# Second-layer products in a form with four sums on each operand, and a third quarter-product first layer, in an attention and mixture-of-experts kernel

## The chip, the cores and the metric

The kernel runs on one core of one Trainium2 chip, as one program. The metric is the device time of an execution in microseconds; the kernel before was run three times. One more execution was taken with the hardware profiler, and every time inside the kernel comes from that one.

## The reference

Eight batches, eight heads of 64, 512 local and 32 global tokens each; the output of the attention is the input of a layer of eight experts over all 4352 tokens.

```python
# attention: global queries see all keys; local queries see the global keys
# and the local keys at a distance of at most 32
s_g   = q_g @ concat(k_g, k_l).T / 8;   out_g = softmax(s_g) @ concat(v_g, v_l)
s_l   = concat(q_l @ k_g.T / 8, where(|i-j| <= 32, q_l @ k_l.T / 8, -1e9))
out_l = softmax(s_l) @ concat(v_g, v_l)
x = concat(out_g, out_l) as [4352, 512]
# experts, E = 8, F = 1024
P = exp(x @ w_gate - max)
8 times: P /= P.sum(1); P /= P.sum(0); P *= N / E
out = sum over e of P[:, e] * (relu(x @ w1[e]) @ w2[e])
```

## The kernel before

The first stage (up to about 340 us) computes the attention and, between its steps, the first layer of experts 0 to 3, whose hidden rows go to DRAM (`hd`). Then the eight normalizations of P run on VectorE while TensorE works off the rest of these first layers. The change lies in the second stage, from about 396 us to the end.

**Units and slots.** The tokens lie in nine groups: 0 to 7 are the 512 local tokens of a batch, group 8 holds the 256 global tokens. In each group the experts are taken in the order 4, 0, 5, 1, 6, 2, 7, 3. One expert on one group is a *unit* i = 8 m + slot; the loop at L1073 goes over the 72 units. Even slots (experts 4 to 7) have their first layer computed here, two units ahead; odd slots (0 to 3) load theirs from DRAM (`load_h`) and scale it by P (`scale_h`, a multiplication of the whole 128x4096 tile h, or of halves of it). For even slots the input is scaled instead (`scale_x`).

**Second layer.** A unit's h is seen as a 2x2 block matrix: rows t1 and t2 (halves of the tokens), columns lo and hi (halves of F, four k-steps each); w2 of an expert as 2x2 blocks as well, kept in `w2c` as seven prepared blocks (`prep_w2c`). Seven products of half size replace eight. `sums` makes their left operands on VectorE, in s (three planes) and in place in h; `product(i, q)` issues product q, eight matmuls of 256 columns with h or s as the stationary operand. Five products stay in their own accumulator banks for the whole group (`ps_fix`) and are added into o once, at the unit that closes the group (slot 7); two use rotating banks and are added after each odd unit (`add`). An addition is one VectorE instruction on 128x512 fp32 from PSUM into o; the first write of a block of o is made by ScalarE. `store` then writes the group out.

**First layer.** `l1` is the plain form: eight rows fm of four matmuls of 512 columns, a ReLU on ScalarE after each. Where `fast(i)` holds (experts 6 and 7 in groups 2 to 7), `Fast` computes it in two halves of F, p = 0 during the even unit i - 2 and p = 1 during the odd unit i - 1, by seven quarter products (four matmuls of 256 columns each) in four steps s0 to s3. ScalarE copies two banks in s0; VectorE makes one addition in s1 (X, L861) and one in s2 (Y, L868), and ReLUs follow in s1, s2 and s3. `sums_x` makes four operands of 128x512 from the scaled x. The stationary operands are seven prepared blocks of w1 (`w1c`), built in group 1 by `prep_w1` from raw blocks and written to DRAM; `wseq` fixes the order in which w1 tiles pass through two buffers.

**Order.** The schedule is manual: every engine runs its instructions in the order in which the program issues them. The loop interleaves them by hand. Three places matter here:

- An even unit that is itself fast (L1084 on) first makes the sums of its k-steps 2 and 3, since these depend on p = 1; k-steps 0 and 1 were summed in the odd unit before.
- In an odd unit with `Fast` (L1148 on), `late` (the even unit before was fast) puts the second half of `scale_h` for unit i + 2 behind the sums.
- The closing odd unit, slot 7, has no `Fast` before: it makes the sums of the next unit first, then the products and their additions (L1171 on).

Of the kernel before, what the change touches and what calls it, by code (L numbers as in the profile page):

```python
# [23 lines left out]
def kernel(  # L24
# [53 lines left out]
    WX = {6: 2, 7: 2}  # L78
# [612 lines left out]
    def prep_w2c(e):  # L691
        w = w2c[e]
        for o, a, b, op in ((0, 1, 4, ALU.add), (5, 1, 2, ALU.add), (6, 3, 4, ALU.add),
                            (2, 2, 4, ALU.subtract), (3, 3, 1, ALU.subtract)):
            tt(w[:, :, o], w[:, :, a], w[:, :, b], op)
# [13 lines left out]
    for j, (e, p) in enumerate((e, p) for e in WX for p in range(2)):  # L709
        wseq.insert(wseq.index((E + 2 * j + 2, None)), (e, "raw", p))  # L710
# [168 lines left out]
    def sums(i, k0=0, k1=HF, part=(0, 1)):  # L879
        if i >= NUN - 1:  # L880
            return
        n = groups[units[i][0]][1]
        t1, t2 = slice(0, n // 2), slice(n // 2, n)
        h = hs[i]
        if i not in ss:
            new_s(i)
        s = ss[i][:, :, k0:k1]
        lo, hi = h[:, k0:k1], h[:, HF + k0 : HF + k1]
        if 0 in part:
            tt(s[:, 0:2, :, 0 : n // 2], lo[:, :, 0:n].rearrange("p k (a t) -> p a k t", a=2),  # L890
               hi[:, :, 0:n].rearrange("p k (a t) -> p a k t", a=2), ALU.add)
            tt(s[:, 2, :, 0 : n // 2], lo[:, :, t1], hi[:, :, t2], ALU.add)
        if 1 in part:
            tt(lo[:, :, t2], lo[:, :, t2], lo[:, :, t1], ALU.subtract)
            tt(hi[:, :, t1], hi[:, :, t1], hi[:, :, t2], ALU.subtract)
# [3 lines left out]
    def rot():  # L899
# [4 lines left out]
    QUARTER = {1: ((0, 0, 1), (1, 1, 1)), 2: ((1, 0, 1), (1, 1, -1)), 3: ((0, 1, 1), (1, 1, 1)),  # L904
               4: ((1, 0, 1), (0, 0, 1)), 5: ((0, 0, -1), (0, 1, 1)), 6: ((1, 1, 1),), 7: ((0, 0, 1),)}
# [6 lines left out]
    def product(i, q):  # L912
        m, e = units[i]
        n = groups[m][1]
        nt = n // P // 2
        first = e == ORDER[0]
        h, s, w = hs[i], ss[i], w2c[e]
        lhs = {1: (s[:, 2], 0), 2: (s[:, 1], 0), 3: (h[:, 0:HF], 0), 4: (h[:, HF:FT], n // 2),
               5: (s[:, 0], 0), 6: (h[:, 0:HF], n // 2), 7: (h[:, HF:FT], 0)}[q]
        if q >= 6 and i % 2 == 0:  # L920
            pm = fixed[q] = ps_rot.tile([P, 512], FP32, tag=rot(), name="pm")
        elif first:
            pm = fixed[q] = ps_fix.tile([P, 512], FP32, tag=f"m{q}", name=f"m{q}")
        else:
            pm = fixed[q]
        for t in range(nt):
            for k in range(HF):
                nc.tensor.matmul(pm[:, HD * t : HD * (t + 1)], lhs[0][:, k, lhs[1] + P * t : lhs[1] + P * (t + 1)],  # L928
                                 w[:, k, q - 1, :], start=(k == 0 and t == 0 and (first if q < 6 else i % 2 == 0)),
                                 stop=(k == HF - 1 and (closes(i) if q < 6 else i % 2 == 1 or closes(i))),  # L930
                                 skip_group_check=True)

    def add(i, q, pm):
        m, e = units[i]
        nt = groups[m][1] // P // 2
        if m not in os_:
            os_[m] = ypool.tile([P, NJ, D], FP32, tag="y", name="o")
        for j, (r, d, sg) in enumerate(QUARTER[q]):
            o = os_[m][:, nt * r : nt * (r + 1), HD * d : HD * (d + 1)]
            p = pm[:, 0 : HD * nt].rearrange("p (t d) -> p t d", d=HD)  # L940
            if (q >= 6 and e == ORDER[1]) or (q in (3, 4) and j == 0):
                nc.scalar.mul(o, p, 1.0 / float(E))
            else:
                nc.vector.scalar_tensor_tensor(out=o, in0=p, scalar=sg / float(E), in1=o, op0=ALU.mult, op1=ALU.add)  # L944
# [4 lines left out]
    def last_pair(i):  # L949
        m, e = units[i]  # L950
        o, h, w = os_[m], hs[i], w2c[e]
        n = groups[m][1]
        lo, hi = h[:, 0:HF, 0:n], h[:, HF:FT, 0:n]
        s = ss[i]
        for c in range(n // P):
            q = slice(P * c, P * (c + 1))
            for d, terms in ((1, ((lo, 2), (s, 4))), (0, ((hi, 3), (s, 1)))):
                pm = ps_rot.tile([P, HD], FP32, tag=rot(), name="pm")
                for t, (a, wi) in enumerate(terms):
                    for k in range(HF):  # L960
                        nc.tensor.matmul(pm, a[:, k, q], w[:, k, wi, :],
                                         start=(t == 0 and k == 0), stop=(t == 1 and k == HF - 1))
                oc = o[:, c, HD * d : HD * (d + 1)]
                nc.vector.scalar_tensor_tensor(out=oc, in0=pm, scalar=1.0 / float(E), in1=oc, op0=ALU.mult, op1=ALU.add)
            for b in range(4 * c, 4 * c + 4):
                eng = (nc.sync, nc.scalar)[b % 2]
                eng.dma_start(out=out[S * b : S * b + Sg, :], in_=o[W * (b % 4) : W * (b % 4 + 1), c, :])
# [105 lines left out]
    for i, (m, e) in enumerate(units):  # L1073
        if i == NUN - 1:
            last_pair(i)
        elif i % 2 == 0:
# [9 lines left out]
            if fast(i + 2):  # L1086
                f = Fast(i + 2, 0)
                if not fast(i):
                    sums(i + 1, part=(0,))
                if fast(i):  # L1090
                    product(i, 3)
                    f.s0()
                    product(i, 4)
                    f.s1()
                    product(i, 5)
                    product(i, 2)
                    sums(i + 1, part=(0,))
                else:
                    f.s0()
                    product(i, 3)  # L1100
                    f.s1()
                    product(i, 4)
                    product(i, 5)
                    sums(i + 1, part=(1,))
                f.s2()
                used.add((i + 2, 0))
                if fast(i):
                    sums(i + 1, part=(1,))
                scale_x(i + 4)
                if not fast(i):  # L1110
                    scale_h(i + 3, 0, HF)
                    product(i, 2)
                product(i, 1)
                f.s3()
                nrot = 0
                product(i, 6)
                product(i, 7)
# [8 lines left out]
            if m > 0:  # L1126
# [9 lines left out]
            for q, fm in ((3, 3), (4, 4), (5, 5), (2, 6), (1, 7), (6, None), (7, None)):  # L1136
# [6 lines left out]
        else:  # L1143
# [4 lines left out]
            if fast(i + 1):  # L1148
                f = Fast(i + 1, 1)
                for q in (6, 7):  # L1150
# [4 lines left out]
                product(i, 3)  # L1155
                f.s0()
                product(i, 4)
                f.s1()
                sums_x(i + 3, (5,))
                product(i, 5)  # L1160
                product(i, 2)
                sums(i + 1, 0, 2, part=(0,))
                f.s2()
                sums(i + 1, 0, 2, part=(1,))
# [3 lines left out]
                product(i, 1)  # L1168
# [6 lines left out]
            for q in (6, 7, 3, 4, 5, 2, 1):  # L1175
                product(i, q)
                if q >= 6 or closes(i):
                    add(i, q, fixed[q])
                if q == 7 and m == 0:
# [34 lines left out]
```

## Time and profile before

| | us |
|---|---|
| three runs: median (lowest to highest) | 1045.08 (1044.48 to 1048.59) |
| the profiled execution, its own time | 1044.08 |
| span of its profile, first to last instruction | 1042.2 |
| TensorE busy in the span | 1015.2 |
| VectorE / ScalarE / GpSimd busy | 868.7 / 513.0 / 139.7 |
| a pair of units with plain first layer, from the chain's first-layer marks (421.99, 441.12) | 19.13 |
| groups 2 to 6, each | 74.95 |
| matmuls of the second layer (L928): number, mean record | 3780, 273 ns |

[...] The granted TensorE clock is 0.995 in the mean. [...]

### The profile page before, as it was taken

How to read it: one execution, taken by the hardware profiler on the slowest of the kernel's cores; microseconds unless marked ns; L12 is line 12 of the kernel's file. 1: busy time of each engine (PE TensorE's matmuls, PEld its weight loads, DVE VectorE, ACT ScalarE, POOL GpSimd, SP SyncE). 2: the span in 40 equal slices, each digit the busy share in tenths (PEclk: the TensorE clock that was granted, in tenths of full speed). 3: DMA queues.
4: the chain of work that ended last, by engine and by line, in shares of the span. 5: the costliest groups of instructions: out<-in, count | busy, mean ns of one | idle time of the engine just before them, and what ended most of it. 6: DMA issues, size and time to landing. Idle time of an engine off the chain costs nothing.

```text
span 1042.2 us, 22693 instructions
## 1 busy us (share of the span) xinstructions
PE 1015.2 (97%) x9142; PEld 728.5 (70%) x9142; DVE 868.7 (83%) x1638; ACT 513.0 (49%) x1296; POOL 139.7 (13%) x227
## 2 busy tenths in 40 slices
PE   7899999999999999999999999999999999999998
PEld 4555555555555466777777877877877878878887
DVE  7687777777776786999889799889899898898895
ACT  7777878787876675223222333333333332332331
POOL 7442423414312102000000000000000000000000
PEclk9899999999999999999999999999999999999999
DMA  9887588988945999946756546454553555464470
GB/s 260 197 217 207 118 273 181 220 232 177 258 136 142 275 261 302 259 143 203 272 194 234 189 153 219 160 189 180 200 189 138 203 187 168 172 218 152 145 260 26
DMA packets 101960, 206.08 MB, mean 198 GB/s; under 512 B 33936, under 2 KB 68192, under 8 KB 90592
## 3 DMA queue, kind: packets, MB, share of 16 engines
q1 hardware_dynamic: 56064, 162.75, 45.1%
q0 software_dynamic: 43184, 32.26, 17.7%
q10 hardware_dynamic: 2608, 9.64, 2.4%
q8 instruction: 71, 1.16, 0.4%
q14 instruction: 33, 0.27, 0.1%
HBM read 168.64 MB, written 57.29 MB: 217 GB/s over the span
## 4 chain that ended last, share of the span: by engine, by line
PE 83%; ACT 8%; DVE 6%; issue 2%; DMA 1%; SPq 0%; POOL 0%; ACTq 0%; DVEq 0%
PE m L928 28%; PE ph L818 15%; PE ph L468 15%; PE pm L928 11%; PE pf L836 7%; ACT Pu L311 4%; DVE Pu L348 3%; PE ptw L359 1%; ACT hT L471 1%; ACT qbd L285 1%; PE pv L157 1%; PE pt L275 1%; DMA vraw<-in_v_l_dram 1%; PE po L380 1%; DVE m L411 1%
## 5 line engine op out<-in xcount | busy, mean ns | idle before, releaser
L468 PE MATMUL ph<-xT,w1e 128*128 128x512 f16 (+1 forms) x1152 | 255.9, 367 | 0.2
L928 PEld LDWEIGHTS <-h 128*128 128x128 f16 x2160 | 211.4, 98 | 36.6
L820 ACT ACTIVATE h<-ph 128x512 f16<-128x512 f32 (+1 forms) x192 | 107.5, 562 | 204.2 <-PE ph L818 202.2
L928 PE MATMUL m<-w2c,s 128*128 128x256 f16 x1620 | 199.9, 273 | 0.0
L928 PEld LDWEIGHTS <-s 128*128 128x128 f16 x1620 | 158.5, 98 | 30.5
L818 PE MATMUL ph<-xs,w1s 128*128 128x512 f16 (+1 forms) x768 | 174.6, 361 | 0.0
L468 PEld LDWEIGHTS <-w1e 128*128 128x128 f16 x1152 | 105.4, 98 | 96.1 <-issue 3.0
L689 DVE TENSOR_TENSOR h<-h,pb 128x2048 f16<-128x2048 f16 (+1 forms) x48 | 152.4, 3175 | 3.8 <-DMA h<-hd 3.7
L689 DVE TENSOR_TENSOR s<-h 128x1024 f16<-128x1024 f16 (+2 forms) x166 | 126.4, 803 | 24.3 <-PE m L928 16.9
L928 PE MATMUL m<-w2c,h 128*128 128x256 f16 x1080 | 137.2, 273 | 0.0
L471 ACT ACTIVATE hT<-ph 128x512 f16<-128x512 f32 (+1 forms) x192 | 104.4, 559 | 47.5 <-PE ph L468 45.2
L928 PE MATMUL pm<-w2c,h 128*128 128x256 f16 x1080 | 123.8, 273 | 0.0
L818 PEld LDWEIGHTS <-w1s 128*128 128x128 f16 x768 | 75.1, 98 | 52.6
L843 ACT ACTIVATE h<-pf 128x512 f16<-128x512 f32 x96 | 55.0, 596 | 84.1 <-PE pf L836 79.9
L311 ACT ACTIVATE Pu<-ms,mx 128x160 f16<-128x160 f32 x224 | 93.6, 420 | 5.2 <-DVE mx L308 2.7
L473 DVE TENSOR_SCALAR hT<-ph 128x512 f16<-128x512 f32 x96 | 66.1, 688 | 31.3 <-PE ph L468 30.5
L689 DVE TENSOR_TENSOR h<-h 128x1024 f16<-128x1024 f16 (+1 forms) x166 | 90.3, 586 | 0.0
L689 DVE TENSOR_TENSOR xs<-xg,pb 128x2048 f16<-128x2048 f16 (+1 forms) x36 | 78.1, 2169 | 12.8 <-DMA pb<-pd 12.8
L947 POOL DMA_DIRECT2D out_dram<-o x8 | 6.1, 758 | 533.3 <-DVE o L944 533.3
L308 DVE CUSTOM_DVE_ANT_0 ms<-sc,mask 128x160 f32<-128x160 f32 x224 | 59.9, 319 | 18.7 <-PE sc L303 18.2
L836 PEld LDWEIGHTS <-w1q 128*128 128x128 f16 x672 | 65.7, 98 | 7.7
L852 ACT COPY pf<-pf 128x512 f32<-128x512 f32 x24 | 13.7, 570 | 81.5 <-PE pf L836 81.5
(165 smaller groups left out, 1225.7 us busy)
## 6 DMA issues: line engine op xcount, KB each, us to landing
h<-hd SPq DMA_DIRECT2D x32, 1024.0 KB
hd<-hT SPq DMA_DIRECT2D x26, 1024.0 KB
w1s<-w1d SPq DMA_DIRECT2D x24, 1024.0 KB
w1q<-w1c SPq DMA_DIRECT2D x24, 896.0 KB
pb<-pd SPq DMA_DIRECT2D x64, 256.0 KB
w2c<-in_moe_w_dram POOLq DMA_DIRECT2D x16, 512.0 KB, 20.1
out_dram<-o POOLq DMA_DIRECT2D x8, 1024.0 KB, 4.6
f<-in_q_l_dram SPq DMA_DIRECT2D x15, 512.0 KB
```

Of the source, the lines that this page charges most:

```text
L308: nc.vector.tensor_tensor_reduce(out=ms[:, ii, :], in0=sc[:, SW * ii : SW * (ii + 1)], in1=mask[:, mi, :], scale=-scale, scalar=BIG, op0=A ...
L311: nc.scalar.activation(out=d["Pu"][:, i, :], in_=ms[:, ii, :], func=AF.Exp, scale=-1.0, bias=d["mx"][:, i : i + 1], accum_out=d["sm"][:, i ...
L348: nc.vector.tensor_tensor(out=d["Pu"][:, i0:i1, 0:KW], in0=d["Pu"][:, i0:i1, 0:KW], in1=d["rs"][:, i0:i1].unsqueeze(2).to_broadcast([P, i1 ...
L468: nc.tensor.matmul(ph[:, 0:n], wts[e][:, dk, P * fm : P * (fm + 1)], xT[m][:, dk, :], start=(dk == 0), stop=(dk == DP - 1))
L471: nc.scalar.activation(out=hT[:, fm, 0:n], in_=ph[:, 0:n], func=AF.Relu)
L473: nc.vector.tensor_scalar(out=hT[:, fm, 0:n], in0=ph[:, 0:n], scalar1=0.0, scalar2=None, op0=ALU.max)
L689: nc.vector.tensor_tensor(out=out, in0=in0, in1=in1, op=op)
L818: nc.tensor.matmul(ph[:, 0:n], w1s[i][:, dk, P * fm : P * (fm + 1)], xss[i][:, dk, 0:n], start=(dk == 0), stop=(dk == DP - 1))
L820: nc.scalar.activation(out=hs[i][:, fm, 0:n], in_=ph[:, 0:n], func=AF.Relu)
L836: nc.tensor.matmul(bank[:, 256 * c : 256 * (c + 1)], self.w[:, self.sta[q], k, P * c : P * (c + 1)], self.mov[q][:, k], start=(first and c ...
L843: nc.scalar.activation(out=self.h[:, k : k + 2, 256 * c : 256 * (c + 1)], in_=bank.rearrange("p (k t) -> p k t", k=2), func=AF.Relu)
L928: nc.tensor.matmul(pm[:, HD * t : HD * (t + 1)], lhs[0][:, k, lhs[1] + P * t : lhs[1] + P * (t + 1)], w[:, k, q - 1, :], start=(k == 0 and ...
```

## The change

The seven products take another form, in which each operand is made with four additions. `sums` has now four parts: S1 = lo t2 + hi t2, S2 = S1 - lo t1, (lo t2 - lo t1) in place, S4 = hi t1 - S2. The rotating products are 2 and 4; the fixed ones 1, 6, 7, 5, 3, in this order. Products 1, 2 and 4 read h as it is; 6 reads S2, 7 the in-place difference, 5 reads S1 and 3 reads S4. `prep_w2c` makes four blocks instead of five.

Expert 4 gets the quarter form in groups 3 to 7 (`WX`): its first layer is then computed during slots 6 and 7 of the group before. So slot 6 becomes an even unit that is fast and is followed by a fast one, and slot 7 an odd unit with `Fast` that also closes its group. Raw blocks of w1 are taken one pair of units earlier, so that expert 4's are built by unit 16.

```diff
-    WX = {6: 2, 7: 2}
+    WX = {6: 2, 7: 2, 4: 3}
...
     def prep_w2c(e):
         w = w2c[e]
-        for o, a, b, op in ((0, 1, 4, ALU.add), (5, 1, 2, ALU.add), (6, 3, 4, ALU.add),
-                            (2, 2, 4, ALU.subtract), (3, 3, 1, ALU.subtract)):
-            tt(w[:, :, o], w[:, :, a], w[:, :, b], op)
+        for o, a, b in ((0, 2, 1), (2, 2, 4), (5, 4, 0), (6, 5, 3)):
+            tt(w[:, :, o], w[:, :, a], w[:, :, b], ALU.subtract)
...
-        wseq.insert(wseq.index((E + 2 * j + 2, None)), (e, "raw", p))
+        wseq.insert(wseq.index((E + 2 * j + 0, None)), (e, "raw", p))
...
-    def sums(i, k0=0, k1=HF, part=(0, 1)):
+    def sums(i, k0=0, k1=HF, part=(0, 1, 2, 3)):
...
-        s = ss[i][:, :, k0:k1]
+        s1, s2, s4 = (ss[i][:, j, k0:k1, 0 : n // 2] for j in range(3))
         lo, hi = h[:, k0:k1], h[:, HF + k0 : HF + k1]
-        if 0 in part:
-            tt(s[:, 0:2, :, 0 : n // 2], lo[:, :, 0:n].rearrange("p k (a t) -> p a k t", a=2),
-               hi[:, :, 0:n].rearrange("p k (a t) -> p a k t", a=2), ALU.add)
-            tt(s[:, 2, :, 0 : n // 2], lo[:, :, t1], hi[:, :, t2], ALU.add)
-        if 1 in part:
-            tt(lo[:, :, t2], lo[:, :, t2], lo[:, :, t1], ALU.subtract)
-            tt(hi[:, :, t1], hi[:, :, t1], hi[:, :, t2], ALU.subtract)
+        for j, (o, a, b, op) in enumerate(((s1, lo[:, :, t2], hi[:, :, t2], ALU.add), (s2, s1, lo[:, :, t1], ALU.subtract),
+                                           (lo[:, :, t2], lo[:, :, t2], lo[:, :, t1], ALU.subtract),
+                                           (s4, hi[:, :, t1], s2, ALU.subtract))):
+            if j in part:
+                tt(o, a, b, op)
...
-    QUARTER = {1: ((0, 0, 1), (1, 1, 1)), 2: ((1, 0, 1), (1, 1, -1)), 3: ((0, 1, 1), (1, 1, 1)),
-               4: ((1, 0, 1), (0, 0, 1)), 5: ((0, 0, -1), (0, 1, 1)), 6: ((1, 1, 1),), 7: ((0, 0, 1),)}
+    ROT, FIX = (2, 4), (1, 6, 7, 5, 3)
...
-        lhs = {1: (s[:, 2], 0), 2: (s[:, 1], 0), 3: (h[:, 0:HF], 0), 4: (h[:, HF:FT], n // 2),
-               5: (s[:, 0], 0), 6: (h[:, 0:HF], n // 2), 7: (h[:, HF:FT], 0)}[q]
-        if q >= 6 and i % 2 == 0:
+        lhs = {1: (h[:, 0:HF], 0), 2: (h[:, HF:FT], 0), 3: (s[:, 2], 0), 4: (h[:, HF:FT], n // 2),
+               5: (s[:, 0], 0), 6: (s[:, 1], 0), 7: (h[:, 0:HF], n // 2)}[q]
+        wi = {1: 1, 2: 3, 3: 4, 4: 6, 5: 0, 6: 5, 7: 2}[q]
+        r = q in ROT
+        if r and i % 2 == 0:
             pm = fixed[q] = ps_rot.tile([P, 512], FP32, tag=rot(), name="pm")
...
                 nc.tensor.matmul(pm[:, HD * t : HD * (t + 1)], lhs[0][:, k, lhs[1] + P * t : lhs[1] + P * (t + 1)],
-                                 w[:, k, q - 1, :], start=(k == 0 and t == 0 and (first if q < 6 else i % 2 == 0)),
-                                 stop=(k == HF - 1 and (closes(i) if q < 6 else i % 2 == 1 or closes(i))),
+                                 w[:, k, wi, :], start=(k == 0 and t == 0 and (i % 2 == 0 if r else first)),
+                                 stop=(k == HF - 1 and (i % 2 == 1 or closes(i) if r else closes(i))),
...
-        for j, (r, d, sg) in enumerate(QUARTER[q]):
-            o = os_[m][:, nt * r : nt * (r + 1), HD * d : HD * (d + 1)]
-            p = pm[:, 0 : HD * nt].rearrange("p (t d) -> p t d", d=HD)
-            if (q >= 6 and e == ORDER[1]) or (q in (3, 4) and j == 0):
-                nc.scalar.mul(o, p, 1.0 / float(E))
+        o00, o01, o10, o11 = (os_[m][:, nt * r : nt * (r + 1), HD * d : HD * (d + 1)] for r in range(2) for d in range(2))
+        p = pm[:, 0 : HD * nt].rearrange("p (t d) -> p t d", d=HD)
+        c = 1.0 / float(E)
+
+        def plus(o, a, sg=1):
+            nc.vector.scalar_tensor_tensor(out=o, in0=p, scalar=sg * c, in1=a, op0=ALU.mult, op1=ALU.add)
+
+        if q in ROT:
+            o, sg = {2: (o00, 1), 4: (o10, -1)}[q]
+            if e == ORDER[1]:
+                nc.scalar.mul(o, p, sg * c)
             else:
-                nc.vector.scalar_tensor_tensor(out=o, in0=p, scalar=sg / float(E), in1=o, op0=ALU.mult, op1=ALU.add)
+                plus(o, o, sg)
+        elif q == 1:
+            nc.scalar.mul(o01, p, c)
+            plus(o00, o00)
+        elif q == 7:
+            plus(o11, o01)
+            tt(o10, o10, o11, ALU.add)
+        else:
+            plus(o01, o01)
+            if q == 5:
+                plus(o11, o11)
...
@@ -1085,36 +1099,36 @@
                 sums(i, 2, 4)
             if fast(i + 2):
                 f = Fast(i + 2, 0)
-                if not fast(i):
-                    sums(i + 1, part=(0,))
                 if fast(i):
+                    product(i, 1)
+                    f.s0()
+                    product(i, 6)
+                    f.s1()
+                    product(i, 7)
+                    product(i, 5)
+                    sums(i + 1, part=(0, 1))
+                    f.s2()
+                    sums(i + 1, part=(2, 3))
+                    scale_x(i + 4)
                     product(i, 3)
+                else:
+                    sums(i + 1, part=(0, 1))
                     f.s0()
-                    product(i, 4)
+                    product(i, 1)
                     f.s1()
+                    product(i, 6)
+                    product(i, 7)
+                    sums(i + 1, part=(2, 3))
+                    f.s2()
+                    scale_x(i + 4)
+                    scale_h(i + 3, 0, HF)
                     product(i, 5)
-                    product(i, 2)
-                    sums(i + 1, part=(0,))
-                else:
-                    f.s0()
                     product(i, 3)
-                    f.s1()
-                    product(i, 4)
-                    product(i, 5)
-                    sums(i + 1, part=(1,))
-                f.s2()
                 used.add((i + 2, 0))
-                if fast(i):
-                    sums(i + 1, part=(1,))
-                scale_x(i + 4)
-                if not fast(i):
-                    scale_h(i + 3, 0, HF)
-                    product(i, 2)
-                product(i, 1)
                 f.s3()
                 nrot = 0
-                product(i, 6)
-                product(i, 7)
+                for q in ROT:
+                    product(i, q)
                 continue
             if i + 2 < NUN:
                 sums(i + 1)
@@ -1123,7 +1137,7 @@
                 h = hs[i + 1]
                 s = ss[i + 1] = xsp.tile([P, HF, n], FP16, tag="xs", name="sl")
                 tt(s, h[:, 0:HF, 0:n], h[:, HF:FT, 0:n], ALU.add)
-            if m > 0:
+            if m > 0 or i == E - 2:
...
-            for q, fm in ((3, 3), (4, 4), (5, 5), (2, 6), (1, 7), (6, None), (7, None)):
+            for q, fm in zip(FIX + ROT, (3, 4, 5, 6, 7, None, None)):
                 product(i, q)
                 if fm is not None:
                     l1(i + 2, fm, ps_rot, rot())
...
             if fast(i + 1):
                 f = Fast(i + 1, 1)
-                for q in (6, 7):
+                for q in ROT:
                     product(i, q)
                     add(i, q, fixed[q])
                 late = fast(i - 1)
                 scale_h(i + 2, *((0, HF) if late else (HF, FT)))
-                product(i, 3)
+                product(i, 1)
                 f.s0()
-                product(i, 4)
+                product(i, 6)
                 f.s1()
                 sums_x(i + 3, (5,))
+                product(i, 7)
                 product(i, 5)
-                product(i, 2)
-                sums(i + 1, 0, 2, part=(0,))
+                sums(i + 1, 0, 2, part=(0, 1))
                 f.s2()
-                sums(i + 1, 0, 2, part=(1,))
+                product(i, 3)
+                if closes(i):
+                    for q in FIX:
+                        add(i, q, fixed[q])
+                    store(m)
+                sums(i + 1, 0, 2, part=(2, 3))
                 if late:
                     scale_h(i + 2, HF, FT)
                 sums_x(i + 3, (7, 6))
-                product(i, 1)
                 f.s3()
                 used.add((i + 1, 1))
                 nrot = 0
                 continue
             if m > 0:
                 sums(i + 1)
-            for q in (6, 7, 3, 4, 5, 2, 1):
+            for q in ROT + FIX:
                 product(i, q)
-                if q >= 6 or closes(i):
+                if q in ROT or closes(i):
                     add(i, q, fixed[q])
-                if q == 7 and m == 0:
+                if q == ROT[-1] and m == 0:
                     sums(i + 1)
```

## The prediction

> **What bounds the kernel now.** I read the page's busy times first, then the windows cut at the groups, the list of waits, and the timeline where one group goes over into the next.
>
> ```profile
> PE 1015.2 (97%) x9142; PEld 728.5 (70%) x9142; DVE 868.7 (83%) x1638; ACT 513.0 (49%) x1296; POOL 139.7 (13%) x227
> ```
> ```profile
> core 0: us, PE busy (x) PEld busy (x) DVE busy (x) ACT busy (x) POOL busy (x), PEclk, DMA share, GB/s
> 402.90:479.40 76.50, 76.50 (x577) 56.35 (x576) 70.83 (x68) 22.09 (x37) 5.64 (x7) 1.00 0.73 206
> 479.40:555.90 76.50, 76.50 (x577) 56.36 (x576) 66.95 (x73) 21.49 (x36) 2.92 (x5) 1.00 0.67 243
> ...
> 705.80:780.80 75.00, 75.00 (x626) 61.06 (x624) 68.54 (x82) 25.40 (x44) 0.75 (x1) 1.00 0.52 187
> ```
> The reader should see that in the second stage TensorE is busy for the whole of every group; from 340 to 1030 us the list of waits has no PE row above 0.5 us. Group 1 (no quarter form) takes 76.5 us, groups with two quarter-form experts 74.95 (the chain's first-layer marks at 555.92 and 630.87). So TensorE's own work is the bound, VectorE's 67 to 69 us of 75 cost nothing, and a change can win only TensorE columns or lose by making TensorE wait.
>
> **What is won.** (76.53 - 74.95) / 2 = 0.79 us for one quarter-form first layer. Expert 4 in groups 3 to 7 makes five: **-3.9 us**. The second layer keeps seven products of the same size. The VectorE instructions it drops (per full unit 1.15 + 0.60 + 2 x 0.60 = 2.95 us of pitch become 4 x 0.60 + 0.12 = 2.52; one of five in the w2 preparation; seven closing additions on VectorE in place of eight) lie beside a full TensorE and bring nothing. Building expert 4's combined w1 adds eight 0.34 us VectorE steps and two stores on POOL's queue in even slots of groups 0 to 2, where VectorE has 6 to 9 us free in a group: nothing; if the reload of it on SP's queue came late at unit 18, about 1 us once. At the end last_pair waited 0.6 us for an addition; nine additions in place of ten take most of it: -0.5.
>
> **What is lost: the order of the queues.** These rows give the pace on VectorE:
>
> ```profile
> L689 DVE TENSOR_TENSOR h<-h,pb 128x2048 f16<-128x2048 f16 x28 | 64.0, 2284 | 1.0 <-DMA h<-hd 0.9
> L944 DVE SCALAR_TENSOR_TENSOR o<-m,o 128x512 f32<-128x512 f32 x64 | 39.8, 684 | 1.2 <-ACT o L942 0.2
> ```
> In the timeline an instruction follows an independent one sooner than its duration: eight o additions take 5.07 us, a pitch of 0.62; 128x512 fp16 0.34; the half scale 2.2. One that reads its predecessor's result costs 0.12 more (t after t 0.46). Now slot 5 into slot 6 of group 6:
>
> ```profile
> 909.93 0.70 DVE L868 TENSOR_TENSOR pf<-pf,c 128x512 f32<-128x512 f32 x1 [0.56 <-issue]
> 910.11 1.04 PE L928 MATMUL m<-w2c,s 128*128 128x256 f16 x8
> 910.54 0.75 DVE L689 TENSOR_TENSOR h<-h 128x512 f16<-128x512 f16 x2
> 910.99 0.60 PE L836 MATMUL pf<-t,w1q 128*128 128x256 f16 x4
> 911.21 2.28 DVE L689 TENSOR_TENSOR h<-h,pb 128x2048 f16<-128x2048 f16 x1
> 911.42 2.75 PE L818 MATMUL ph<-xs,w1s 128*128 128x512 f16 x12
> ...
> 913.41 1.02 DVE L689 TENSOR_TENSOR s<-h 128x1024 f16<-128x1024 f16 x2
> ```
> Call E the end of the odd unit on TensorE (here 911.42). Addition Y (L868) starts at E - 1.49, because TensorE's quarter product releases it; so VectorE's queue from there on has a fixed start. It then does two steps on h, the half scale, and reaches the late sums of the even unit at E + 1.99. TensorE had three l1 rows and two products that need no sum in front of it, 6.0 us, and never noticed.
>
> *Slot 5 to 6 after, groups 2 to 6.* Slot 6 is now followed by a quarter-form unit, so TensorE goes product 1 (0.87, as from 910.11 to 910.99), s0 (two quarter products of 0.44), and product 6, whose first two k-steps (0.22) use early sums: at E + 1.96 it needs S2 of k 2 and 3. VectorE is at E + 1.99 with three new sums_x steps still ahead of it (7, 6, then 4: 1.2), then S1 0.34 and S2 0.46, and 0.1 until TensorE sees it: E + 4.1. **TensorE waits 2.15 us.** Queued behind on TensorE is everything; nothing else can fill it.
>
> *Slot 7 to slot 0 after, into groups 3 to 7.* Slot 7 closes the group and now also runs s0 to s3 of expert 4. Y begins at E - 1.49 and takes 0.62; product 1's addition runs to E - 0.25. The next adds into o01, which ScalarE must write first, behind both ReLUs of the quarter form (Y's ends near E + 0.05) and 0.6 us of its own: VectorE resumes at E + 0.75. Six more instructions (products 6, 7 with the o10 sum, 5 twice, 3) at 0.62 and two dependences: E + 4.7. S4 and its companion for k 0 and 1, 0.67: 5.4. The late half scale 2.2: 7.6. S1, S2 of k 2 and 3: 8.4, seen at 8.5. TensorE meanwhile has three l1 rows (2.6, as from 911.42 to 914.01), product 1 (0.87), l1 (0.87) and two k-steps: E + 4.55. **It waits 3.95 us.** The fp32 sum of two SBUF tiles has no row; nearest are 0.44 us (128x272, both SBUF) and 0.70 (128x512, one PSUM); I take 0.62, as the adds of its size. Before, this slot made the sums of slot 0 ahead of the additions, so nothing with a near deadline stood behind the additions.
>
> Elsewhere I find cover. Slot 3 to 4 has no late half scale; the same count gives S2 at E + 1.9 against E + 1.96, within 0.1. After the long wait VectorE has slot 0's eight l1 and slots 1 and 2 to recover. Product banks, x and w1q arrive as before.
>
> Five boundaries x (2.15 + 3.95) = **+30.5**. The lower end, with no dependence gaps, is 28; the upper, every VectorE instruction at its full recorded duration (1.3 us more at a boundary), about 37. [...]
>
> **The clock.** Waits of this size are new to this stage, and the first stage shows what they can do:
>
> ```profile
> 29.20:32.60 3.40, 1.47 (x42) 1.24 (x42) 3.31 (x13) 3.35 (x14) 1.56 (x2) 1.00 1.12 237
> 32.60:36.00 3.40, 2.75 (x52) 2.31 (x52) 2.66 (x9) 0.74 (x3) 0.86 (x2) 0.50 0.95 190
> 36.00:39.40 3.40, 2.62 (x30) 2.26 (x29) 3.02 (x19) 3.40 (x15) 1.83 (x3) 0.50 0.68 178
> 39.40:42.80 3.40, 3.40 (x36) 1.69 (x36) 2.33 (x7) 2.46 (x7) 1.09 (x2) 0.50 1.06 195
> 42.80:46.30 3.50, 3.50 (x22) 1.72 (x21) 1.60 (x8) 2.48 (x8) 2.60 (x3) 0.99 0.94 210
> ```
> After a stretch in which TensorE was busy 1.47 of 3.40 us (43%) the granted clock fell to one half and came back after a stretch that was full; 8.7 to 12.1 us, with 56%, lost nothing. The changes lie 10.2 us apart, three stretches of 3.4. A wait of 3.95 us takes at least 58% of one such stretch wherever the stretches lie, and 68% or more for four positions in five; the short wait takes at most 63%. I count four falls after the five long waits, none after the short ones, and one full stretch at half speed each, 1.7 us: **+6.8**; bounds 0 and 5 x 2.9 = 14.5 (1.2 us more where a partly idle stretch comes first and doesn't restore it). [...]
>
> **Sum.** The profiled execution took 1044.08 us (span 1042.2), 1.0 under the median of 1045.08. 1044.1 - 3.9 - 0.5 + 30.5 + 6.8 = 1077.0, and on the median's footing 1078.
>
> **The rivals.**
> - *Both waits, clock holds:* 1078 - 6.8 = 1071. For it: TensorE is dense around each wait, unlike at 29 us. [...] Together 0.2, half each. [...]
> - *No slowdown; the waits are covered.* TensorE stays the bound and only the columns count: 1045.1 - 3.9 - 0.5 = 1040.7, which is 0.4% faster. It decides at one point: S2 of k 2 and 3 must be there by E + 1.96 in slot 6 and E + 4.55 in slot 0. That needs VectorE to run those sums ahead of the late half scale and the additions; in the trace it runs strictly in the order of the program (L868, h, h<-h,pb, s), so 0.06.
> - *One wait only:* the long one alone 1045.1 - 4.4 + 19.8 = 1060.5, the short one alone 1051.5. The closing additions could flow better than I queue them. 0.08.
> - *Worse clock or backlog:* the clock also falls after short waits, or stays down three stretches as at 32.6: 1071 + 5 x 5.1 = 1096. 0.08.
>
> **How the numbers follow.** My forecast has 0.58. The range goes from the long wait alone (1060) to both bounds together (1071 + 14.5 + 6.5 = 1092); it leaves out the covered case, the short wait alone and the worst clock. A measurement of this kernel can tell about 0.5% (5.2 us) from no change. The covered case at -0.4% falls inside that: 0.02 for faster, 0.06 for the same, and 0.92 for slower.
>
> **What the changed profile would show.** Right: PE rows appear in the list of waits, lines of product waiting for DVE s, ten in all, near 2.1 and 4.0 us; beside the clock, group 2 lasts 74.2 + 2.1 us, groups 3 to 6 74.2 + 6.1, and group 7, whose slots 6 and 7 keep plain first layers, some 4 more than now; clock 0.5 for some 3.4 us after long waits. Group 1 keeps 76.5. Wrong: group lengths of 74.2 us and no PE wait, or idle time at other slots (4, or product 3's S4), or the clock at 1.00 all through.

## The result and the profile after

The changed kernel takes 1085.05 us (median of 4 runs, 1081.91 to 1087.67) against 1044.78 us of the kernel before in the same comparison: ratio 1.0376, 95% interval 1.0338 to 1.0414. Its profiled execution took 1084.16 us, 40.1 more than that of before.

The page's span and busy times, then all rows of its list of waits, from 340 us on, in which TensorE waited (engine, line, releaser: us in total, times, longest):

```profile
span 1082.3 us, 23078 instructions
...
PE 1024.6 (95%) x9262; PEld 744.2 (69%) x9262; DVE 861.2 (80%) x1694; ACT 516.2 (48%) x1307; POOL 140.8 (13%) x229
```
```profile
PE m L926 <- DVE s L689: 30.5, 10, 4.2
PE pt L1024 <- DVE lt L1019: 0.5, 1, 0.5
PE ph L817 <- DMA w1s<-w1d: 0.5, 1, 0.5
```

There was no row of products waiting for sums before; now there are ten waits: five at slot 6 (groups 2 to 6) and five at slot 0 (groups 3 to 7). VectorE is less busy than before (861 against 869 us) and yet holds TensorE up: it is the order of its queue, not its load. The timeline at slot 6 and at slot 0, from group 3 into group 4 (start, duration, engine):

```profile
694.68 2.29 DVE L689 TENSOR_TENSOR h<-h,pb 128x2048 f16<-128x2048 f16 x1
696.63 0.38 PE L926 MATMUL m<-w2c,s 128*128 128x256 f16 x2
697.22 0.95 DVE L689 TENSOR_TENSOR t<-xs,t 128x512 f16<-128x512 f16 x2
698.54 0.42 DVE L689 TENSOR_TENSOR s<-s,h 128x512 f16<-128x512 f16 x1
699.02 0.83 PE L926 MATMUL m<-w2c,s 128*128 128x256 f16 x6 [2.01 <-DVE s L689]
...
715.46 2.75 PE L817 MATMUL ph<-xs,w1s 128*128 128x512 f16 x12
719.79 0.38 PE L926 MATMUL m<-w2c,s 128*128 128x256 f16 x2
721.25 2.29 DVE L689 TENSOR_TENSOR h<-h,pb 128x2048 f16<-128x2048 f16 x1
723.91 0.42 DVE L689 TENSOR_TENSOR s<-s,h 128x512 f16<-128x512 f16 x1
724.39 1.09 PE L926 MATMUL m<-w2c,s 128*128 128x256 f16 x6 [4.22 <-DVE s L689]
```

In both places product 6 issues its two early k-steps (x2), stops, and goes on (x6) when S2 (s<-s,h) is there; the late half scale (h<-h,pb) and, at 697.22, the sums_x steps stand ahead of S2. The windows after the second wait show the clock (columns as before: stretch, its length, busy time of PE, PEld, DVE, ACT, POOL, then the granted clock):

```profile
721.00:724.20 3.20, 0.00 (x0) 0.00 (x0) 3.17 (x4) 0.00 (x0) 0.73 (x1) 1.00 0.61 250
724.90:728.10 3.20, 3.20 (x13) 1.67 (x12) 2.60 (x5) 0.60 (x1) 0.00 (x0) 0.50 0.73 193
728.40:731.80 3.40, 3.40 (x26) 2.29 (x24) 2.97 (x3) 1.13 (x2) 0.00 (x0) 1.00 0.94 395
```

After the idle stretch TensorE runs a full one at half speed: 13 matmuls where the next holds 26 (of other sizes). Six times in this execution the clock fell in the second stage before its end: at each of the five long waits (from 639.5, 724.8, 806.7, 892.1 and 974.0 us) and after one short one (782.9); four of them for 3.4 us, two for 6.8, together 27.3 us. The two that lasted 6.8 us (639.5 and 806.7) began while TensorE was still waiting:

```profile
639.50:642.90 3.40, 1.87 (x8) 1.19 (x9) 3.33 (x8) 0.00 (x0) 0.00 (x0) 0.50 1.03 296
642.90:646.30 3.40, 3.40 (x14) 1.81 (x12) 1.92 (x4) 0.60 (x1) 0.00 (x0) 0.50 0.87 294
```

As the cost I count, an estimate, half of the time in which TensorE worked: a row of four l1 matmuls took 1.71 us in the fall at 724.8 us (725.27 to 726.98) and 0.86 us behind it (728.47 to 729.33). TensorE waited for 1.5 us of each of the two long falls, so 24.2 of the 27.3 us were work at half speed, and the clock cost 12.1 us: 1.7 for a short fall, 2.6 for a long one.

The account. From the first product of a group to that of the next, and without the waits and this cost of the clock, group 2 takes 74.3 us and groups 3 to 6 take 74.4 to 74.5, against 74.95 before. So 2.5 us of TensorE columns were won, not 3.9. (With half of the whole 6.8 us as the cost, groups 3 and 5 would come out at 73.7, unlike 4 and 6.) -2.5 (columns) + 30.5 (waits) + 12.1 (clock) = +40.1, and +40.1 was measured. Small differences elsewhere cancel to 0.2 us: 0.6 more in group 1 and 0.3 more in group 7, 0.4 less ahead of the groups and 0.3 less at the end.

### The profile page after: what moved, and what is told of

It reads as the page before. It is cut to its first block, busy times and chain, and to the rows that moved or that the text cites. A ratio compares the mean times of both kernels' runs of the same rounds, so it can differ in the third digit from the quotient of the medians.

```text
span 1082.3 us, 23078 instructions
## 1 busy us (share of the span) xinstructions
PE 1024.6 (95%) x9262; PEld 744.2 (69%) x9262; DVE 861.2 (80%) x1694; ACT 516.2 (48%) x1307; POOL 140.8 (13%) x229
## 4 chain that ended last, share of the span: by engine, by line
PE 77%; DVE 12%; ACT 7%; issue 2%; DMA 0%; ACTq 0%; DVEq 0%
PE m L926 26%; PE ph L468 14%; PE pm L926 11%; PE ph L817 10%; PE pf L835 9%; ACT Pu L311 3%; DVE Pu L348 3%; DVE h L689 2%; DVE o L941 1%; PE ptw L359 1%; DVE s L689 1%; ACT hT L471 1%; ACT qbd L285 1%; PE pt L275 1%; PE pv L157 1%
## 5 line engine op out<-in xcount | busy, mean ns | idle before, releaser
L926 PE MATMUL m<-w2c,s 128*128 128x256 f16 x1620 | 212.0, 275 | 30.5 <-DVE s L689 30.5
L819 ACT ACTIVATE h<-ph 128x512 f16<-128x512 f32 (+1 forms) x152 | 83.7, 552 | 193.7 <-PE ph L817 183.5
L926 PE MATMUL m<-w2c,h 128*128 128x256 f16 x1080 | 145.7, 278 | 0.0
L817 PE MATMUL ph<-xs,w1s 128*128 128x512 f16 (+1 forms) x608 | 140.3, 366 | 0.5 <-DMA w1s<-w1d 0.5
L842 ACT ACTIVATE h<-pf 128x512 f16<-128x512 f32 x136 | 77.7, 596 | 129.2 <-PE pf L835 111.5
L835 PEld LDWEIGHTS <-w1q 128*128 128x128 f16 x952 | 93.2, 98 | 10.8
L817 PEld LDWEIGHTS <-w1s 128*128 128x128 f16 x608 | 60.8, 100 | 43.6 <-issue 3.6
L835 PE MATMUL pf<-xs,w1q 128*128 128x256 f16 x544 | 76.0, 273 | 0.0
L689 DVE TENSOR_TENSOR s<-h 128x1024 f16<-128x1024 f16 (+1 forms) x88 | 49.5, 562 | 32.6 <-PE m L926 22.0
L851 ACT COPY pf<-pf 128x512 f32<-128x512 f32 x34 | 19.4, 570 | 106.3 <-PE pf L835 106.3
```

The costliest lines, as they stand in the source:

```text
L689: nc.vector.tensor_tensor(out=out, in0=in0, in1=in1, op=op)
L817: nc.tensor.matmul(ph[:, 0:n], w1s[i][:, dk, P * fm : P * (fm + 1)], xss[i][:, dk, 0:n], start=(dk == 0), stop=(dk == DP - 1))
L819: nc.scalar.activation(out=hs[i][:, fm, 0:n], in_=ph[:, 0:n], func=AF.Relu)
L835: nc.tensor.matmul(bank[:, 256 * c : 256 * (c + 1)], self.w[:, self.sta[q], k, P * c : P * (c + 1)], self.mov[q][:, k], start=(first and c ...
L842: nc.scalar.activation(out=self.h[:, k : k + 2, 256 * c : 256 * (c + 1)], in_=bank.rearrange("p (k t) -> p k t", k=2), func=AF.Relu)
```

## The experiments

Two theories were to be told apart from mine (order of VectorE's queue at slots 6 and 0, plus the clock): that one half of the change is slow by itself, and that VectorE has no room. Ratios are to the kernel before in the same comparison.

**1. The form alone.** `WX = {6: 2, 7: 2}` in the changed kernel.

> The new form of the second layer alone: expert 4 keeps its plain first layer. Theory (the loss comes from slots 6 and 0, where a quarter-form slot follows a late half scale or the closing additions, and the new form has one free product in front): no such slot exists without expert 4, so TensorE waits nowhere, groups 2 to 6 keep 74.95 us, and the time is the kernel before's within 1.5 us, about 1044. Rival (the form itself is slower, by its chained sums or its longer additions): waits of TensorE for DVE s in every group, and 1050 us or more.

1043.98 us, ratio 1.0002 (0.9993 to 1.0012). The trace has no wait of a product.

```profile
PE 1014.8 (97%) x9142; PEld 728.6 (70%) x9142; DVE 833.1 (80%) x1621; ACT 507.3 (49%) x1287; POOL 139.4 (13%) x227
```

VectorE is 36 us less busy than before and the time is the same: within this interval the form alone costs nothing and, beside a full TensorE, brings nothing.

**2. Expert 4's quarter form alone,** on the old form of the products. The raw blocks of w1 are taken earlier, as in the changed kernel, and product 1 of the closing unit goes ahead of the additions instead of behind sums_x:

```diff
-    WX = {6: 2, 7: 2}
+    WX = {6: 2, 7: 2, 4: 3}
...
                 f.s2()
+                if closes(i):
+                    product(i, 1)
+                    for q in (3, 4, 5, 2, 1):
+                        add(i, q, fixed[q])
+                    store(m)
                 sums(i + 1, 0, 2, part=(1,))
```

> Expert 4's quarter form alone, with the old form of the products; slot 7's additions stand, as in the changed kernel, between Y and the sums of k-steps 0 and 1. The old form has two free products and s0, s1 in front of the first sum. Theory: in slot 6 the late sums are there at E + 3.9 us against a need at E + 3.7, wait 0.2; in slot 0 E + 7.8 against E + 6.3, wait 1.5. Five boundaries: +8.5, columns -3.9, the clock holds: about 1049 us. Rival (the quarter form at slot 0 costs by itself, through its VectorE and ScalarE work or its loads, whatever the form): 1075 us or more, as in the changed kernel.

1064.61 us, ratio 1.0192 (1.0175 to 1.0209): between the two expectations, so neither held as it stood.

```profile
PE m L928 <- DVE s L689: 12.9, 5, 2.6
PE pf L836 <- DVE pf L861: 3.4, 4, 0.9
PE pf L836 <- DVE pf L868: 2.1, 5, 0.4
```

The wait at slot 6 is gone, as said. The one at slot 0 is 2.6 us where I had 1.5: VectorE began the additions 1.3 us after Y, behind two first writes by ScalarE, where I had let them follow at once. New are waits for X and Y (L861, L868), 5.5 us together, and the clock fell once (3.4 us). So the quarter form costs about half of the loss with the old products too. The other half comes only with both: 0 and +20 alone, +40 together. That it comes from the new form's single free product in front is argued from the order of the queue; some 10 us of it are the clock (12.1 against 1.7).

**3. Sums first.** In the changed kernel the late half scale of slot 5 moves behind the sums of slot 6, and the additions and the late half scale of slot 7 behind the sums of slot 0:

```diff
                 sums(i, 2, 4)
+                if e == ORDER[0]:
+                    for q in FIX:
+                        add(i - 1, q, fixed[q])
+                    store(m - 1)
+                    scale_h(i + 1, HF, FT)
+                if fast(i - 2) and fast(i + 2):
+                    scale_h(i + 1, HF, FT)
...
-                if closes(i):
-                    for q in FIX:
-                        add(i, q, fixed[q])
-                    store(m)
...
-                if late:
+                if late and not closes(i) and not fast(i + 3):
                     scale_h(i + 2, HF, FT)
```

> The changed kernel with two places of the VectorE queue moved: in slots 5 the late half scale goes behind the sums of the even slot, and in slots 7 the closing additions and the late half scale do. Nothing else differs. Theory (order alone): the sums are there at E + 1.9 in slot 6 and E + 1.1 in slot 0, the half scale delays X by 0.3 us in slot 6; TensorE waits about 0.4 us at a boundary, the clock holds, and the time is 1044.1 - 3.9 - 0.5 + 2 = 1042 us, 0.3% under the kernel before. Rival (VectorE has no room: its work moves on and waits come up elsewhere): most of the 30 us of waits stays, 1065 us or more.

1074.68 us, ratio 1.0294 (1.0259 to 1.0328). My expectation was wrong: 1042 was expected. The ten waits are gone from their places, and others have come; the clock fell twice, each time with a wait of 2.2 us for w1q:

```profile
PE pf L835 <- DMA w1q<-w1c: 12.1, 7, 2.2
PE m L926 <- DVE s L689: 8.4, 5, 2.4
PE pf L835 <- DVE pf L860: 6.1, 5, 1.2
```

A new kind, a load. On SP's queue the loads stand in the order pb, h, w1q:

```profile
697.71 0.32 SPq L751 DMA_DIRECT2D pb<-pd  x1
698.12 0.38 SPq L803 DMA_DIRECT2D h<-hd  x1
698.60 0.38 SPq L728 DMA_DIRECT2D w1q<-w1c  x1
```

The even slot began at 692.93; pb went out at 697.71, just after the moved half scale (695.40, 2.29 us) let go of its pb buffer, and w1q stood behind it.

**4. The same, with the w1 load first on SP's queue** in every even slot (`load_w1(used)` moved above `load_pbs(i)`).

> The sums-first kernel of the first set (1074.7 us; TensorE waited 12.1 us for loads of w1q and 14.5 us for VectorE), with the w1 load issued first in every even slot, ahead of the loads of pb. Theory (the moved half scale holds its pb buffer longer, the next pb load waits for it at the head of SP's queue, and the w1q load stands behind): the waits for w1q go, and with them two falls of the clock: about 1060 us, with VectorE's waits left. Rival (the w1q load is slow by itself, through contention): 1070 us or more and the waits for w1q stay.

1062.46 us, ratio 1.0188 (1.0164 to 1.0212). No wait for w1q is left and the clock stays at 1.00 up to the last units; waits for sums and for X remain, at slot 2:

```profile
PE m L926 <- DVE s L689: 10.1, 5, 2.2
PE pf L835 <- DVE pf L860: 6.1, 5, 1.2
```

That settles the load: it was late by its place in the queue.

**5. Matmuls in the wait.** Four rows of matmuls that nobody reads, before product 6 in slot 0 of the changed kernel:

```diff
+                if q == 6 and fast(i) and e == ORDER[0]:
+                    for fill in range(4):
+                        ph = ps_rot.tile([P, 512], FP32, tag=rot(), name="fill")
+                        for dk in range(DP):
+                            nc.tensor.matmul(ph, w1s[i + 2][:, dk, P * fill : P * (fill + 1)], xss[i + 2][:, dk, 0:512],
+                                             start=(dk == 0), stop=(dk == DP - 1))
                 product(i, q)
```

> The changed kernel with four more rows of matmuls (3.5 us, results read by nobody) on TensorE in slot 0 of groups 3 to 7, just before product 6, where it waits 4.1 us. They fit into the wait, so they cost no time themselves; TensorE is busy there. Theory (about 12 of the 40 us lost are the clock, which falls because of the idle time): the clock stays at 1.00 after slot 0 and the time falls to about 1073 us although more work is done; the fall after one short wait (1.7) may stay. Rival (the clock is not set by idle time, or its half speed is hidden by waits that follow): 1084 us or more.

1078.46 us, ratio 1.0328 (1.0312 to 1.0344): faster than the changed kernel, but by 5 us (by the ratios; 6.6 by the medians) and not by 12. After slot 0 the clock no longer fell. It fell after four of the five short waits instead, where it had been one, and so by the same count cost 6.8 us in place of 12.1; and a wait for a load of w1s in group 1 is 2.0 us where it was 0.5. That leaves 3.8 us, and the two profiled executions lie 3.5 apart. The stretch with the first of these waits and the one behind it:

```profile
614.40:617.70 3.30, 1.29 (x13) 0.92 (x11) 3.16 (x7) 1.07 (x2) 0.00 (x0) 1.00 0.24 71
617.80:621.10 3.30, 3.30 (x18) 2.38 (x16) 0.80 (x3) 0.60 (x1) 0.00 (x0) 0.50 0.86 340
```

In the first of the two TensorE was idle for 2.01 us, 59% of 3.41, and the clock fell: a wait of 2.0 us was enough here. In the changed kernel the short wait before the fall at 782.9 us took 59% of a stretch as well; the other four took at most 44, 44, 50 and 53% of one, and the clock held after them. Where the other three waits with a fall lie in this run's stretches is not shown.

**6. Order mended at slot 6 only:** the scale split 3/4 early and 1/4 late, and S1, S2 ahead of sums_x.

```diff
-                scale_h(i + 2, *((0, HF) if late else (HF, FT)))
+                scale_h(i + 2, *((0, FT - 2) if late else (HF, FT)))
...
-                sums_x(i + 2, (4,))
-                sums(i, 2, 4)
+                sums(i, 2, 4, part=(0, 1))
+                if fast(i - 2):
+                    sums_x(i + 2, (7, 6))
+                sums(i, 2, 4, part=(2, 3))
+                sums_x(i + 2, (4,))
...
-                    scale_h(i + 2, HF, FT)
-                sums_x(i + 3, (7, 6))
+                    scale_h(i + 2, FT - 2, FT)
+                if not late:
+                    sums_x(i + 3, (7, 6))
```

> The changed kernel with VectorE's order mended around slot 6: the half scale of a late slot is split 3/4 early and 1/4 late in place of 1/2 and 1/2, and in slot 6 S1 and S2 of k-steps 2 and 3 come ahead of the sums_x steps 7, 6 and 4. Slot 0's late part is shorter too. Theory: S2 is there at E + 1.85 in slot 6, against E + 1.96, so the short waits vanish; in slot 0 the sums come 1.1 us sooner, wait 3.0: 1044.1 - 4.4 + 15 + clock (five falls, 1.7 to 3.4 each, 12) = 1067 us. Rival (the earlier scale delays X and moves the wait to s2): waits of TensorE for DVE pf of the same size, 1075 us or more.

1064.87 us, ratio 1.0203 (1.0184 to 1.0221), 2 us under what was expected: five waits of 2.98 us are left, all at slot 0, and four falls of the clock, 17.1 us in all, of which TensorE worked for 15.3.

**7. The same with three rows of matmuls in slot 0's wait,** to settle the clock without the short waits.

> The kernel with the order mended around slot 6 (1064.9 us; TensorE waits 3.0 us in slot 0 of five groups, and its clock fell four times, 17.1 us at half speed), with three more rows of matmuls (2.6 us, read by nobody) on TensorE in slot 0 just before product 6. Theory (the clock falls because of the idle time): idle time of 0.4 us is left there, no fall, and the time drops by half of 17.1 us, 8.5, to about 1056 us though TensorE does more. Rival (the falls are not due to the wait): 1065 us, or 1078 if the rows came on top.

1056.93 us, ratio 1.0120 (1.0104 to 1.0135): 7.9 us less than without the rows (8.7 by the ratios; 6.6 between the two profiled executions), where half of 15.3 is 7.7. Of that, 0.9 us goes to a longer wait for w1s in group 1. The row of waits for sums, and a window over most of groups 3 to 7, each first without the rows of matmuls and then with them:

```profile
PE m L926 <- DVE s L689: 14.9, 5, 3.0
PE m L926 <- DVE s L689: 2.0, 5, 0.4
```
```profile
632.00:1010.00 378.00, 363.09 (x3096) 305.11 (x3094) 327.06 (x441) 127.63 (x228) 3.79 (x5) 0.98 0.51 182
632.00:1010.00 378.00, 376.04 (x3224) 314.65 (x3222) 331.69 (x449) 130.30 (x234) 3.80 (x5) 1.00 0.53 187
```

The second stage has no fall up to its last two microseconds. With 60 more matmuls the kernel is faster; the clock's share is shown.

**8. Five l1 rows ahead of product 6 in slot 0,** nothing else.

```diff
+            ahead = fast(i) and e == ORDER[0]
...
                 product(i, q)
-                if fm is not None:
+                if ahead and q == 1:
+                    for f in range(3, FT):
+                        l1(i + 2, f, ps_rot, rot())
+                if fm is not None and not ahead:
                     l1(i + 2, fm, ps_rot, rot())
```

> The changed kernel; in slot 0 after a quarter-form first layer the five remaining l1 rows go ahead of product 6 instead of between the products. Same instructions, another order on TensorE. Theory: product 6 then comes 3.46 us later, at E + 8.0, against sums seen at about E + 8.7; the wait at slot 0 falls from 4.1 to 0.7 us, the one at slot 6 stays at 2.0, with clock falls after some of these: 1044.1 - 4.4 + 5 x 2.7 + about 7 = 1060 us. Rival (VectorE is behind by an amount that grows with any cover): the wait stays near 4 us, 1080 us or more.

1067.64 us, ratio 1.0231 (1.0207 to 1.0255). That is 7.6 us over what was expected. The waits at the two places are as computed, 0.60 and 2.01 us, and the clock fell only once; but 1.2 us for X, five times, and some 0.2 for sums, three times, came up at slot 2, which the long wait had hidden.

**9. Both orders, 6 and 8.**

> Both changes of order together: five l1 rows ahead of product 6 in slot 0, and the split scale with S1 and S2 ahead of sums_x in slot 6. Theory: sums at about E + 7.6 against E + 8.0 in slot 0 and E + 1.85 against E + 1.96 in slot 6: no wait over 0.3 us, the clock stays at 1.00, only the columns count: 1044.1 - 3.9 - 0.5 = 1040 us, 0.4% under the kernel before. Rival (VectorE, at 91% of the group, is the bound once TensorE has no slack): waits come up at other slots, 1046 us or more.

1053.13 us, ratio 1.0096 (1.0081 to 1.0111): expected was 1040, and the rival's sign, 1046 or more with waits at other slots, came instead. The clock holds; waits of 1 and 1.2 us remain at slot 2. VectorE's rows from slot 0 to slot 2 say why:

```profile
719.67 2.29 DVE L689 TENSOR_TENSOR xs<-xg,pb 128x2048 f16<-128x2048 f16 x1 [2.24 <-DMA pb<-pd]
...
723.67 4.42 DVE L689 TENSOR_TENSOR h<-h,pb 128x4096 f16<-128x4096 f16 x1
728.00 0.68 DVE L689 TENSOR_TENSOR s<-h 128x1024 f16<-128x1024 f16 x1
```

VectorE stood still for 2.24 us for a load of pb, with scale_h and the sums of slot 2 behind it. That load went out at 713.47 us, just after the late quarter scale (712.22, 1.22 us) had let go of its pb buffer. So waits came up elsewhere, as the rival had it, but behind a load and not for want of room; experiment 10 puts that to the test.

**10. In slot 0 also the loads of h and w1 ahead of those of pb on SP, and scale_h of slot 3 ahead of scale_x of slot 4 on VectorE.**

```diff
-            load_pbs(i)
+            if not ahead:
+                load_pbs(i)
...
             load_h(i + 3)
             load_w1(used)
+            if ahead:
+                load_pbs(i)
...
+            if ahead:
+                scale_h(i + 3)
             scale_x(i + 4)
```

> The kernel with both changes of order (1053 us; left are waits at slot 2, about 2.4 us in each of groups 3 to 7, behind 2.2 us in which VectorE waits in slot 0 for a pb load that stands ahead of the load of h on SP's queue), with two more changes in slot 0: SP issues the loads of h and w1 ahead of the two pb loads, and VectorE scales h of slot 3 ahead of x of slot 4. Theory: VectorE goes on without its wait, S2 of slot 2 comes about 1.3 us ahead of its need, no wait of TensorE over 0.3 us is left, and the time is 1041 us, 0.3% under the kernel before. Rival (VectorE at 91% has no room for three quarter-form slots): waits of 1 us and more stay at some slot, 1046 us or more.

1041.93 us, ratio 0.9974 (0.9963 to 0.9985): some 42 us under the changed kernel by the ratios, and 0.26% under the kernel before: little, but its whole interval lies below 1. All rows of the list of waits with TensorE, from 340 us on, and three windows of a group's length:

```profile
PE pt L1024 <- DVE lt L1019: 0.5, 1, 0.5
PE ph L817 <- DMA w1s<-w1d: 0.5, 1, 0.5
PE pl L455 <- DVE hT L473: 0.4, 1, 0.4
```
```profile
632.00:706.00 74.00, 73.98 (x648) 63.26 (x647) 68.15 (x92) 26.25 (x48) 0.77 (x1) 1.00 0.57 196
706.00:780.00 74.00, 73.98 (x648) 63.08 (x646) 68.14 (x92) 26.25 (x47) 0.77 (x1) 1.00 0.57 196
780.00:854.00 74.00, 73.98 (x648) 63.11 (x646) 68.15 (x92) 26.25 (x47) 0.75 (x1) 1.00 0.57 196
```

TensorE is full again, with VectorE at 92%. Group 3 starts at 631.62 and group 4 at 705.95: 74.33 us against 74.95 before. All arithmetic of the change is in; only orders, and the place where one scale is cut in two, differ from the changed kernel. So VectorE had the room: it is not the bound, and the loss was order. Which of the two changes of this last step removed the waits at slot 2 was not told apart.

## Why the prediction came out as it did

- *What is won, -3.9:* over-sized. In the changed kernel the groups won 2.5 us beside the waits. In the last kernel, where nothing waits, group 2 won the 0.79 that was counted, and groups 3 to 6 take 74.33 us where the count gave 74.16: 3.3 in all. Why a later group wins less stays open.
- *The last pair, -0.5:* its wait of 0.6 us is gone from the list; a new wait of 0.5 us for a load of w1s in group 1 took that back.
- *The wait at slot 6, 2.15 us:* 2.01 measured.
- *The wait at slot 0, 3.95 us:* 4.05 to 4.22 measured. One step was off: I let product 1's addition run ahead of ScalarE's first write; the trace (E = 715.46) has VectorE idle 1.15 us until that write and all seven additions after it, from E + 0.67.

```profile
716.13 2.02 DVE L941 SCALAR_TENSOR_TENSOR o<-m,o 128x512 f32<-128x512 f32 x3 [1.15 <-ACT o L950]
```

The rest of that queue ran at the pitches I took (three additions in 2.0 us; the half scale, 2.29 us long, was followed 2.20 us after its start), not at full durations, so the upper end of 37 did not come about.
- *The sum of waits, +30.5:* 30.5 in the trace. The mechanism was right; that the sum agrees to a tenth is luck, since the short wait was a little shorter than computed and the long one a little longer.
- *The clock, +6.8:* mis-sized; it was 12.1, within the bounds. I counted four falls of one stretch each after long waits and none after short ones. There were six: every long wait and one short, and two of them lasted two stretches. This 5.3 us and the 1.4 us of columns that were not won make the 7 us between 1078 and 1085. That short waits cost nothing had no row behind it: the row at 29.20 us lost the clock at 57% idle, and by the prediction's own count a short wait takes up to 63% of a stretch. All six falls here came after stretches that were partly busy, 10 to 41% of the time, as the row at 29.20 us was (43%).
- *The signs:* group 2 came out at 76.3 us (76.3 said), groups 3 to 6 at 80.5 to 80.7 beside the clock (80.3 said), and group 7 some 4 longer. Group 1 was to keep 76.5 and took 77.2.
- *The covered case, 1040.7:* not how the change runs, but what it could be: the last experiment reaches 1041.9 by meeting the condition named there, S2 in time at both slots. The prediction asked only for those two; slot 2, w1q and pb came on top.
- *Elsewhere I find cover:* true for the changed kernel, but the long wait was part of the cover. With it gone, slot 2 waited.

## What to carry to other kernels

Where one engine is full, price a change by the first instruction of that engine that needs something new, and count what stands ahead of the supplier on its own queue from the last event that the full engine itself releases; here that gave ten waits to within 0.3 us. A form with fewer additions, which alone cost nothing here, can be dearer beside another change if its first products need them sooner. Moving a step later also moves the release of its buffers, and any load behind them (in experiment 3 this left seven waits for w1q, 2.2 us at the longest): look at every queue before the wait is called gone, and ask again which wait the removed one had hidden.

## What the runs showed of the hardware

*When the granted clock fell.* In the profiles of the kernel before and of the changed kernel the changes of the granted clock lie whole multiples of 3.413 us apart (3.41, 6.83, 10.24, 20.48, 54.61, 78.51 us and so on); a stretch is a piece of 3.413 us between such points. In the second stage of the changed kernel, up to its last units, the clock fell to one half six times, after stretches in which TensorE had been idle for 73, 87, 59, 73, 81 and 90% of the time; the idlest stretches after which it held had 53, 50 and 44%. In the first stage the two lie otherwise: the clock fell after 57% (kernel before, stretch from 29.2 us) and after 50 and 54% (changed kernel, stretches from 4.6 and 28.5 us). By waits: it fell after all five of 4.05 to 4.22 us (changed kernel) and after four of the five of 2.98 us (experiment 6); of the five of 2.01 us it fell after one in the changed kernel, after four in experiment 5 and after one in experiment 8.

*How long, and at what cost.* Of the six falls in the changed kernel four lasted 3.41 us, and TensorE worked all through them; the two that lasted 6.83 us had it idle for 1.5 us at their start. At one half a row of four 512-column matmuls took 1.71 us, at full clock 0.86. In experiment 7 matmuls that nobody reads, put into the wait, made the kernel 7.9 us faster (1064.87 to 1056.93 us).
